# Second block of layer 2: a step's seven products of w_ch1 in one go, then all 36 matmuls of w_ch2

## The chip, the core and the metric

The kernel runs on one core of a Trainium2 chip. The metric is the time of one execution in device microseconds (us). Engines are called PE (TensorE, the matrix engine; PEld its weight loads), DVE (VectorE), ACT (ScalarE), POOL (GpSimd) and SP (the queue that issues the DMAs).

## What is computed

A retention layer feeds a gated layer, whose result x feeds a plain one. The change lies in the last of the three:

```python
def _moe2_ref(x, g_ln, w_ch1, w_ch2):
    mu = np.mean(x, axis=-1, keepdims=True)
    var = np.mean((x - mu) ** 2, axis=-1, keepdims=True)
    xn = (x - mu) / np.sqrt(var + 1e-06) * g_ln
    ch = np.maximum(xn @ w_ch1, 0.0) @ w_ch2
    return (x + ch).astype(np.float32)
```

x is (4, 576, 512), w_ch1 is 512 by 2048 and w_ch2 is 2048 by 512, all in float32.

## The kernel before

The 2304 rows of x are worked off in NB = 3 blocks of TB = 6 row tiles (768 rows). A block has NQ = 8 steps; a step makes 256 of the 2048 hidden columns. Steps are counted through, s = 0 to 23: block 0 is steps 0 to 7, block 1 steps 8 to 15, block 2 steps 16 to 23.

Precision comes from splitting each float32 operand into a high and a low part of type fp32r; `mm3` (lines 135 to 137) multiplies them in three matmuls, high by high, high by low, low by high.

*The products of a step.* xn @ w_ch1 is formed by a scheme with seven products in place of eight (`HIDDEN`: the features' mixture, the accumulator, and whether the product is the first or last of it). One call of `product` is one of them: two times `mm3`, six matmuls of 384 columns. Between them DVE and ACT add and subtract what has come out, in the tiles `u` and `t`, and `relu` (line 1173) makes the four quarters of the hidden tile `h`: ACT writes the high part (line 1175), DVE the low part (line 1176). Quarter (i, hh) is number q = 2 i + hh. `hidden(s)` issues the seven products in four parts, (0, 5), (1, 2), (3, 4) and (6,), and yields behind each.

*The projection.* `project(s, q)` multiplies quarter q by w_ch2: three row tiles times `mm3`, nine matmuls of 512 columns, called a portion here, 36 in four portions for a step. They add into six PSUM banks that hold the block's output rows for its eight steps. Of the eight banks two are left for products; `bank()` takes the one that has been free longest. At the block's last step DVE adds the residual row (loaded by `load_rest`) and SP stores the row.

*The order.* The main loop runs over s and, within it, over q = 0 to 3. In each turn stand: a part of step s's products, then one portion of the step before (so steps 1 to 16 hold 36 matmuls of w_ch2 in four portions), then the loading, splitting (`split_w2`, `split_w1`), saving (`save_w2`, `save_w1`) and fetching (`fetch_w1`) of weights, then `ahead`, the work on the next block: loading rows, normalising them (`norm`), loading them turned (`load_features`), scaling them (`scale_features`, ACT line 1015), and, in its turns 24 to 31, the differences (`mix_features`, POOL line 1029) and splits (`split_features`, ACT line 1036 and POOL line 1037) that make the mixtures. A turn of `ahead` is called a tick; `ahead` has 32 in a block. From step 8 on `turning` also brings w_ch2 into the form that block 2 wants: POOL differences (line 961), ACT casts into staging tiles (line 964), POOL low parts (line 967), and SP saves them (line 970).

Block 2 (`hidden_kept`) keeps its hidden tiles and is not projected step by step. Each engine carries out its instructions in the order in which this code issues them; nothing reorders them.

Of the kernel before, what the change touches and what calls it, by code (L numbers as in the profile page):

```python
# [27 lines left out]
KE = E // 128  # L28
# [73 lines left out]
def kernel(  # L102
# [1070 lines left out]
    def relu(s, i, v):  # L1173
        t = h_t[s, i] = h_at[i][s % len(h_at[i])]
        act.activation(out=t[:, 0], in_=v, func=ACTF.Relu)  # L1175
        dve.scalar_tensor_tensor(  # L1176
            out=t[:, 1], in0=v, scalar=0.0, in1=f(t[:, 0]), op0=ALU.max, op1=ALU.subtract
        )

    def hidden(s):  # L1180
# [5 lines left out]
        for part in ((0, 5), (1, 2), (3, 4), (6,)) if s else ((5, 0, 2, 4), (1,), (3,), (6,)):  # L1186
            for w in part:
# [7 lines left out]
                elif w in (0, 5):  # L1195
                    dve.tensor_tensor(out=u, in0=v, in1=u, op=ALU.add)
                elif w == 2 or w == 4:
                    dve.tensor_tensor(out=t, in0=v, in1=u if w == 2 else t, op=ALU.add)
                    if w == 4:
                        relu(s, 3, t)  # L1200
                else:
                    if w != 1:
                        y = u if w == 6 else v
                        dve.tensor_tensor(out=y, in0=v, in1=u, op=ALU.add)  # L1204
                        v = y
                    relu(s, {1: 0, 3: 2, 6: 1}[w], v)
                if last:
                    free(bk[a])
            yield

    def hidden_kept(s):
# [46 lines left out]

    def project(s, q):

        blk, p = divmod(s, NQ)
        i, h = divmod(q, 2)
        t = h_t.pop((s, q))
        if p == 0 and q == 0:
            o_t[blk] = [bank() for j in range(TB)]
        first, last = p == 0 and i == 0, p == NQ - 1 and i == 1
        w = w2_at[i]
        for j in reversed(range(TB // 2)):
            c = slice(j * 128, (j + 1) * 128)
            ps = o_t[blk][h * TB // 2 + j]  # L1270
            mm3(ps, t[:, 0, c], t[:, 1, c], w[:, 0], w[:, 1], first, last)
            if last:
                n = blk * TB + h * TB // 2 + j

                o = row_tile()
                dve.tensor_tensor(
                    out=turned_row(o), in0=ps.rearrange("p (f k c) -> p f k c", k=KE, c=32),
                    in1=o_s.pop(n).rearrange("p (f k c) -> p f k c", k=KE, c=32), op=ALU.add,
                )
                free(ps)  # L1280
                store_row(n, o)

# [111 lines left out]
    def ahead(blk, q):  # L1394
# [3 lines left out]
        n = (blk + 1) * TB  # L1398
        if q == 1 and blk:
            for j in reversed(range(TB // 2, TB)):  # L1400
                load_rest((blk - 1) * TB + j)
        if blk + 1 < NB:
# [21 lines left out]
            if q >= 24 and q != 28:  # L1424
                if q > 24:
                    next(feat[0], None)
                next(feat[1])
        if q == 4 * NQ - 1:
            for j in reversed(range(TB // 2)) if blk + 1 < NB else range(TB):
                load_rest(blk * TB + j)  # L1430
            if blk + 1 == NB:
                o_s[None] = row_tile()

# [29 lines left out]
    for s in range(NB * NQ):  # L1463
        if s == NK:
            keep()
        steps = hidden(s) if s < NK else hidden_kept(s)
        for q in range(4):
            next(steps)
            if 0 < s <= NK:
                project(s - 1, q)  # L1470
            if s >= NQ:
                next(turns, None)

            if q == 0 and s > 1:
                split_w2(2 * s - 1)
            if q == 1 and s > 1:
                load_w2(2 * s + 1)
                save_w2(2 * s - 1)
            if q == 2 and s:
                split_w2(2 * s)  # L1480
            if q == 3 and s:
                load_w2(2 * s + 2)
                save_w2(2 * s)
            if s and q == 2:
# [24 lines left out]
            else:  # L1509
                fetch_w1(s + 2, q - 1)  # L1510
    for _ in multiply_kept(NB - 1):
        pass
# [60 lines left out]
```

## Time and profile before

| | |
|---|---|
| median of 3 runs | 657.69 us (656.92 to 658.03) |
| the profiled execution | 658.18 us, its span 656.2 us |
| PE busy | 646.8 us, 99% of the span |
| DVE, ACT, POOL busy | 455.0, 316.0, 321.6 us |
| block 0 of layer 2 in the span | about 282 to 399 us, its last portions of w_ch2 in step 8 |
| block 1 | about 399 to 525 us, its last 36 matmuls of w_ch2 in step 16, to 541 us |

The span is cut into stretches for reading. A matmul's printed length reaches from its start to its modelled end and overlaps the next one, so the distance from start to start is what it costs. "Idle before" names what an engine waited for before an instruction. A DMA's time is from its issue on SP to its landing.

### The profile page before, as it was taken

To read this page: it belongs to the slowest core of one execution; us is meant where nothing else is said; L and a number is where in the kernel's file an instruction comes from. 1 tells how busy PE (TensorE), PEld (TensorE's weight loads), DVE (VectorE), ACT (ScalarE), POOL (GpSimd) and SP (SyncE) were. 2 spreads that over 40 slices of the span, in tenths; PEclk is the share of its full clock that TensorE was granted. 3 is DMA by queue.
4 is the path that set the end of the run, shared out by engine and by line. 5 is a ranking of instruction groups with operands and counts; after the bars stand their busy time and mean duration, and the time that the engine had idled before them with its cause. 6 is when DMAs were issued, how large, how long until landed. Compare 5 with 4: busy or idle time off the path is not lost.

```text
span 656.2 us, 12551 instructions
## 1 busy us (share of the span) xinstructions
PE 646.8 (99%) x4422; PEld 591.2 (90%) x4422; DVE 455.0 (69%) x906; ACT 316.0 (48%) x656; POOL 321.6 (49%) x315
## 2 busy tenths in 40 slices
PE   8998999999999999999999999999999999999997
PEld 5998899899889889899888999888988899999996
DVE  4698779789989885868888533555533345458894
ACT  4556795365286466434453533233535313335443
POOL 2467868225326528945655793265559743310000
PEclk9999999999999999999999999999999999999999
DMA  8999447777797695489896867799999699999634
GB/s 306 383 368 371 166 111 213 252 238 233 259 298 232 189 242 145 151 312 384 319 309 238 274 205 261 247 366 387 347 332 360 216 295 350 371 379 405 243 129 161
DMA packets 99264, 181.22 MB, mean 276 GB/s; under 512 B 9857, under 2 KB 46849, under 8 KB 97410
## 3 DMA queue, kind: packets, MB, share of 16 engines
q1 hardware_dynamic: 99202, 180.42, 81.5%
q8 instruction: 35, 0.57, 0.3%
q14 instruction: 27, 0.22, 0.1%
HBM read 122.97 MB, written 56.62 MB: 274 GB/s over the span
## 4 chain that ended last, share of the span: by engine, by line
PE 71%; DVE 3%; ACT 3%; DMA 1%; issue 1%; POOL 1%; SPq 0%; POOLq 0%; ACTq 0%; DVEq 0%
PE b L137 20%; PE b L136 20%; PE b L135 20%; PE b L864 4%; PE b L1341 3%; PE b L1342 2%; DVE c L163 1%; DMA raw<-in_w_ch_dram 1%; ACT t L695 1%; PE b L798 1%; POOL vnl L721 1%; PE b L797 0%; ACT t L692 0%; ACT raw L160 0%; DVE bs L669 0%
## 5 line engine op out<-in xcount | busy, mean ns | idle before, releaser
L137 PE MATMUL b<-fe,w 128*128 128x384 f32 x336 | 113.1, 337 | 0.0
L135 PE MATMUL b<-fe,w 128*128 128x384 f32 x336 | 112.9, 336 | 0.0
L136 PE MATMUL b<-fe,w 128*128 128x384 f32 x336 | 112.7, 335 | 0.0
L137 PE MATMUL b<-w,h 128*128 128x512 f32 (+1 forms) x270 | 98.1, 363 | 0.0
L136 PE MATMUL b<-w,h 128*128 128x512 f32 (+1 forms) x270 | 98.0, 363 | 0.0
L135 PE MATMUL b<-w,h 128*128 128x512 f32 (+1 forms) x270 | 96.8, 358 | 0.0
L945 POOL TENSOR_TENSOR w<-raw_w,w 128x512 fp32r<-128x512 f32 x30 | 39.6, 1320 | 59.0 <-ACT w L944 53.3
L135 PEld LDWEIGHTS b<-fe,w 128*128 128x128 f32 x336 | 63.1, 188 | 3.0
L136 PEld LDWEIGHTS b<-fe,w 128*128 128x128 f32 x336 | 63.1, 188 | 2.8
L137 PEld LDWEIGHTS b<-fe,w 128*128 128x128 f32 x336 | 63.0, 188 | 0.0
L137 PEld LDWEIGHTS b<-w,h 128*128 128x128 f32 x270 | 51.0, 189 | 7.6
L160 ACT ACTIVATE raw<-raw 128x512 f32<-128x512 f32 x44 | 29.9, 679 | 56.2 <-DVE b L158 49.3
L136 PEld LDWEIGHTS b<-w,h 128*128 128x128 f32 x270 | 50.9, 189 | 6.3 <-POOL w L945 0.2
L135 PEld LDWEIGHTS b<-w,h 128*128 128x128 f32 x270 | 51.0, 189 | 6.0 <-issue 0.2
L1175 ACT ACTIVATE h<-b 128x384 fp32r<-128x384 f32 x32 | 15.7, 492 | 83.8 <-DVE b L1204 54.1
L665 POOL TENSOR_TENSOR st<-st,par 128x1 f32<-128x1 f32 x36 | 22.1, 617 | 52.7 <-DVE st L664 52.2
L1176 DVE SCALAR_TENSOR_TENSOR h<-b,h 128x384 fp32r<-128x384 f32 x32 | 17.8, 556 | 30.9 <-ACT h L1175 30.9
L137 PE MATMUL b<-w_sg,vnl 128*128 128x288 f32 x128 | 37.8, 295 | 0.2 <-POOL vnl L721 0.2
L135 PE MATMUL b<-w_sg,vnh 128*128 128x288 f32 x128 | 37.8, 295 | 0.0
L137 PE MATMUL b<-xt_hi,w_in 128*128 128x288 f32 x128 | 37.7, 295 | 0.0
L136 PE MATMUL b<-w_sg,vnh 128*128 128x288 f32 x128 | 37.7, 295 | 0.0
L136 PE MATMUL b<-xt_lo,w_in 128*128 128x288 f32 x128 | 37.7, 294 | 0.0
(199 smaller groups left out, 1700.8 us busy)
## 6 DMA issues: line engine op xcount, KB each, us to landing
w<-ws_dram SPq DMA_DIRECT2D x96, 256.0 KB, 4.8
raw<-in_w_ch_dram SPq DMA_DIRECT2D x32, 512.0 KB, 5.0
ws_dram<-w SPq DMA_DIRECT2D x16, 896.0 KB, 7.4
w<-wb_dram SPq DMA_DIRECT2D x14, 1024.0 KB, 5.6
qv<-in_attn_dram SPq DMA_DIRECT2D x15, 576.0 KB, 6.8
w_dram<-c SPq DMA_DIRECT2D x32, 256.0 KB, 3.1
wb_dram<-fe SPq DMA_DIRECT2D x32, 256.0 KB, 5.1
kk<-in_attn_dram SPq DMA_DIRECT2D x15, 544.0 KB, 7.7
```

The source lines that it names most:

```text
L135: pe.matmul(ps, lh, rh, start=first, stop=False, skip_group_check=True)
L136: pe.matmul(ps, lh, rl, start=False, stop=False, skip_group_check=True)
L137: pe.matmul(ps, ll, rh, start=False, stop=last, skip_group_check=True)
L160: act.activation(out=f(w1), in_=f(w1), func=ACTF.Square)
L163: dve.scalar_tensor_tensor(out=f(c), in0=f(w1), scalar=F64_LEAST ** 2, in1=f(r), op0=ALU.is_ge, op1=ALU.mult)
L665: pool.tensor_tensor(out=st[:, 4:5], in0=st[:, 3:4], in1=col(par, O_MH), op=ALU.pow)
L864: pe.matmul(ps, g, wo[k][:, w], start=done[0] == 1, stop=done[0] == 3 * KE, skip_group_check=True)
L945: pool.tensor_tensor(out=t[:, 1], in0=raw, in1=f(t[:, 0]), op=ALU.subtract)
L1175: act.activation(out=t[:, 0], in_=v, func=ACTF.Relu)
L1176: dve.scalar_tensor_tensor(out=t[:, 1], in0=v, scalar=0.0, in1=f(t[:, 0]), op0=ALU.max, op1=ALU.subtract)
L1341: pe.matmul(ps, e[:, 0, x], t, start=begin, stop=False, skip_group_check=True)
L1342: pe.matmul(ps[:, 0:256], e[:, 1, x], t[:, 0:256], start=False, stop=end, skip_group_check=True)
```

## The change

In block 1 a step's seven products are issued in one go (`hidden_once`, in the order w = 0, 5, 1, 2, 4, 3, 6), and all 36 matmuls of w_ch2 of the same step behind them, quarters 3, 2, 0, 1. Within a quarter the nine matmuls run over the three row tiles for each of the three high and low pairs, where `mm3` did the three pairs for each row tile; the block's last step keeps `mm3`. The low part of `h` becomes a function of its own (`relu_low`), so that it may come later; for quarter 0 DVE first copies the product to a new tile `z`, and the bank is given back. The products of step 7 are projected behind step 7's last turn, so that step 8 starts with nothing left over, and step 16 has nothing to project. w_ch2's two splits of a step stand behind its second product and in the third turn, its loads and one of its saves behind the second product. The residual rows are loaded in ticks 28 and 29 (before: three in tick 31 and three in tick 1 of the next block). The work of the four turns, `ahead` included, is issued behind the portions as before, but a turn holds no products any more.

The number of matmuls and of DMAs is the same; DVE has eight copies more.

```diff
     def relu(s, i, v):
         t = h_t[s, i] = h_at[i][s % len(h_at[i])]
         act.activation(out=t[:, 0], in_=v, func=ACTF.Relu)
+
+    def relu_low(s, i, v):
+        t = h_t[s, i]
         dve.scalar_tensor_tensor(
             out=t[:, 1], in0=v, scalar=0.0, in1=f(t[:, 0]), op0=ALU.max, op1=ALU.subtract
         )
...
+    def hidden_once(s):
+        u = t2.tile([128, TH], F32, tag="u", name="u")
+        t = t2.tile([128, TH], F32, tag="v", bufs=1, name="t")
+        z = t2.tile([128, TH], F32, tag="z", bufs=1, name="z")
+        bk = {}
+        for w in (0, 5, 1, 2, 4, 3, 6):
+            x, a, first, last = HIDDEN[w]
+            if first:
+                bk[a] = bank()
+            product(s, bk[a], w, x, first, last)
+            v = bk[a][:, 0:TH]
+            if w == 0:
+                act.copy(u, v)
+            elif w == 1:
+                relu(s, 0, v)
+                dve.tensor_copy(out=z, in_=v)
+            elif w == 2 or w == 4:
+                dve.tensor_tensor(out=t, in0=v, in1=u if w == 2 else t, op=ALU.add)
+                if w == 4:
+                    relu(s, 3, t)
+            elif w == 3:
+                dve.tensor_tensor(out=v, in0=v, in1=u, op=ALU.add)
+                relu(s, 2, v)
+                relu_low(s, 3, t)
+            else:
+                dve.tensor_tensor(out=u, in0=v, in1=u, op=ALU.add)
+                if w == 6:
+                    relu(s, 1, u)
+            if last and w != 3:
+                free(bk[a])
+            if w == 5:
+                yield
+        relu_low(s, 2, bk[2][:, 0:TH])
+        free(bk[2])
+        relu_low(s, 0, z)
+        relu_low(s, 1, u)
+        yield
...
-    def project(s, q):
+    def project(s, q, begin=0):
...
-        first, last = p == 0 and i == 0, p == NQ - 1 and i == 1
+        first, last = p == 0 and i == begin, p == NQ - 1 and i != begin
         w = w2_at[i]
-        for j in reversed(range(TB // 2)):
+        js = list(reversed(range(TB // 2)))
+        for x, y in ((0, 0), (0, 1), (1, 0)) if begin and not last else ():
+            for j in js:
+                pe.matmul(
+                    o_t[blk][h * TB // 2 + j], t[:, x, j * 128:(j + 1) * 128], w[:, y], start=first and x == y,
+                    stop=False, skip_group_check=True,
+                )
+        for j in () if begin and not last else js:
...
-        if q == 1 and blk:
-            for j in reversed(range(TB // 2, TB)):
-                load_rest((blk - 1) * TB + j)
+        if q in (28, 29) and blk + 1 < NB:
+            for j in reversed(range(TB // 2)):
+                load_rest(blk * TB + (q - 28) * TB // 2 + j)
...
-        steps = hidden(s) if s < NK else hidden_kept(s)
+        if s < NQ:
+            steps = hidden(s)
+        elif s < NK:
+            steps = hidden_once(s)
+            next(steps)
+            split_w2(2 * s)
+            if s == NQ:
+                split_w2(2 * s + 1)
+            load_w2(2 * s + 2)
+            load_w2(2 * s + 3)
+            if s > NQ:
+                save_w2(2 * s + 1)
+            next(steps)
+        else:
+            steps = hidden_kept(s)
         for q in range(4):
-            next(steps)
-            if 0 < s <= NK:
+            if NQ <= s < NK:
+                project(s, (3, 2, 0, 1)[q], 1)
+            else:
+                next(steps)
+            if 0 < s < NQ:
                 project(s - 1, q)
             if s >= NQ:
                 next(turns, None)
 
-            if q == 0 and s > 1:
-                split_w2(2 * s - 1)
...
+            if s < NQ:
+                if q == 0 and s > 1:
+                    split_w2(2 * s - 1)
...
+            else:
+                if q == 1:
+                    save_w2(2 * s)
+                    if s == NQ:
+                        save_w2(2 * s + 1)
+                if q == 2:
+                    split_w2(2 * s + 3)
...
+        if s == NQ - 1:
+            split_w2(2 * s + 1)
+            load_w2(2 * s + 3)
+            for q in range(4):
+                project(s, q)
```

How the order moves, at three places. First PE, at the end of step 8 of block 1 before (b are PSUM banks, fe the features, w_3466 and w_3467 the high and low part of w_ch1, w_3373 the tile of w_ch2): the last three matmuls of a portion and the first three of the next product.

```order
L135 MATMUL b_76<-w_3373,h 128x512
L136 MATMUL b_76<-w_3373,h 128x512
L137 MATMUL b_76<-w_3373,h 128x512
L135 MATMUL b_78<-fe,w_3466 128x384 [waits DMAHW0_49]
L136 MATMUL b_78<-fe,w_3466 128x384
L137 MATMUL b_78<-fe,w_3467 128x384 [waits DMAHW1_49]
```

Now, at the end of the products of the first such step: the last three matmuls of the seventh product and the first nine of the 36.

```order
L135 MATMUL b_81<-fe,w_3371 128x384
L136 MATMUL b_81<-fe,w_3371 128x384
L137 MATMUL b_81<-fe,w_3372 128x384
L1316 MATMUL b_77<-w_3373,h 128x512 [waits Activation_49]
L1316 MATMUL b_78<-w_3373,h 128x512
L1316 MATMUL b_80<-w_3373,h 128x512
L1316 MATMUL b_77<-w_3373,h 128x512 [waits Pool_49]
L1316 MATMUL b_78<-w_3373,h 128x512
L1316 MATMUL b_80<-w_3373,h 128x512
L1316 MATMUL b_77<-w_3373,h 128x512 [waits DVE_49]
L1316 MATMUL b_78<-w_3373,h 128x512
L1316 MATMUL b_80<-w_3373,h 128x512
```

Behind a product stood nine matmuls of w_ch2 four times a step; now 36 stand together once.

Second DVE, in a step of block 1 before: from the sum for w = 5 to the sum for w = 6.

```order
L1196 TENSOR_TENSOR u<-b_78,u 128x384 [waits PE_49,Activation_49]
L1176 SCALAR_TENSOR_TENSOR h<-b_77,h 128x384 [waits Activation_49]
L1198 TENSOR_TENSOR t<-b_78,u 128x384 [waits DVE_49,PE_49]
L1204 TENSOR_TENSOR b_78<-b_78,u 128x384 [waits PE_49]
L1176 SCALAR_TENSOR_TENSOR h<-b_78,h 128x384 [waits Activation_49]
L1198 TENSOR_TENSOR t<-b_77,t 128x384 [waits DVE_49,PE_49]
L1176 SCALAR_TENSOR_TENSOR h<-t,h 128x384 [waits Activation_49]
```

The same piece now, to the end of the step's products.

```order
L1243 TENSOR_TENSOR u<-b_79,u 128x384 [waits PE_49,Activation_49]
L1233 COPY z<-b_81 128x384 [waits Activation_49]
L1235 TENSOR_TENSOR t<-b_79,u 128x384 [waits DVE_49,PE_49]
L1235 TENSOR_TENSOR t<-b_81,t 128x384 [waits DVE_49,PE_49]
L1239 TENSOR_TENSOR b_79<-b_79,u 128x384 [waits PE_49]
L1179 SCALAR_TENSOR_TENSOR h<-t,h 128x384 [waits Activation_49]
L1243 TENSOR_TENSOR u<-b_81,u 128x384 [waits DVE_49,PE_49]
L1179 SCALAR_TENSOR_TENSOR h<-b_79,h 128x384 [waits Activation_49]
L1179 SCALAR_TENSOR_TENSOR h<-z,h 128x384
L1179 SCALAR_TENSOR_TENSOR h<-u,h 128x384 [waits Activation_49]
```

The copy to z (L1233) is new, waits for ACT and reads b_81, the bank that w = 1 left and that w = 4 takes two products later (the row with t<-b_81,t); the low parts (L1179) stand later.

Third ACT, before, in the ticks 24 to 27 of block 1: the casts of the mixtures (L1036) up to the copy to u that begins step 15 (L1194).

```order
L1036 CAST fe<-x 128x768
L1175 ACTIVATE h<-b_79 128x384 [waits PE_49,Activation_49]
L1036 CAST fe<-mix 128x768 [waits Pool_49]
L1175 ACTIVATE h<-b_78 128x384 [waits DVE_49]
L1175 ACTIVATE h<-t 128x384 [waits DVE_49]
L944 CAST w_3373<-raw_w_5411 128x512 [waits DMAHW2_49,DMAHW3_49,PE_49,Activation_49]
L1036 CAST fe<-mix 128x768 [waits Pool_49]
L1175 ACTIVATE h<-u 128x384 [waits DVE_49,Activation_49]
L1036 CAST fe<-mix 128x768 [waits Pool_49]
L1194 COPY u<-b_78 128x384 [waits PE_49]
```

The same ticks now, from the last ReLU of step 14 to the first of step 15 (L1230 is the copy to u).

```order
L1175 ACTIVATE h<-u 128x384 [waits DVE_49,Activation_49]
L1036 CAST fe<-x 128x768
L1036 CAST fe<-mix 128x768 [waits Pool_49]
L944 CAST w_3373<-raw_w_5497 128x512 [waits DMAHW3_49,DMAHW2_49,DMAHW4_49,PE_49,Activation_49]
L1036 CAST fe<-mix 128x768 [waits Pool_49] x2
L1230 COPY u<-b_81 128x384 [waits PE_49]
L944 CAST w_3373<-raw_w_5495 128x512 [waits DMAHW3_49,DMAHW1_49,Activation_49]
L1175 ACTIVATE h<-b_81 128x384 [waits DVE_49,PE_49,Activation_49]
```

The four casts stood between the step's own ReLUs; now all four stand in a row in front of the next step's copy to u. On POOL the instructions behind the first of them are:

```order
L1037 TENSOR_TENSOR fe<-x,fe 128x768 [waits Activation_49]
L1029 TENSOR_TENSOR mix<-x,mix 128x768 [waits Pool_49]
L1037 TENSOR_TENSOR fe<-mix,fe 128x768 [waits Activation_49]
L945 TENSOR_TENSOR w_3373<-raw_w_5497,w_3373 128x512 [waits DMAHW3_49,DMAHW4_49,DMAHW2_49,Activation_49]
L1029 TENSOR_TENSOR mix<-x,mix 128x768 [waits Pool_49]
L1037 TENSOR_TENSOR fe<-mix,fe 128x768 [waits Activation_49]
```

The second difference (the lower L1029) is what the last of the four casts waits for.

## Rows read from the trace of the kernel before

**Rows 1.** The page, busy time of each engine

```profile
PE 646.8 (99%) x4422; PEld 591.2 (90%) x4422; DVE 455.0 (69%) x906; ACT 316.0 (48%) x656; POOL 321.6 (49%) x315
```

**Rows 2.** Timeline of PE, a step of block 1: start us, length us, instruction

```profile
407.64 0.33 PE L135 MATMUL b<-fe,w 128*128 128x384 f32 x1
...
408.70 0.33 PE L135 MATMUL b<-fe,w 128*128 128x384 f32 x1
...
409.74 0.39 PE L135 MATMUL b<-w,h 128*128 128x512 f32 x1
...
411.82 0.33 PE L135 MATMUL b<-fe,w 128*128 128x384 f32 x1
```

**Rows 3.** Timeline of PE, end of the layer before

```profile
279.31 2.88 PE L864 MATMUL b<-w_out,grem 128*128 128x512 f32 x12
282.03 0.33 PE L135 MATMUL b<-fe,w 128*128 128x384 f32 x1
```

**Rows 4.** Timeline of PE, at its one gap in the stretch

```profile
425.69 0.50 PE L136 MATMUL b<-w,h 128*128 128x512 f32 x1
426.03 0.40 PE L137 MATMUL b<-w,h 128*128 128x512 f32 x1
```

**Rows 5.** Timelines of PE and ACT in block 2, a product and its ReLU

```profile
550.98 0.33 PE L137 MATMUL b<-fe,w 128*128 128x384 f32 x1
551.35 0.49 ACT L1229 ACTIVATE kept<-b 128x384 f32<-128x384 f32 x1 [1.48 <-PE b L137]
```

**Rows 6.** Groups by line, 405 to 530 us: instruction, count, busy us, mean ns, idle before

```profile
L1175 ACT ACTIVATE h<-b 128x384 fp32r<-128x384 f32 x16 | 7.9, 492 | 51.1 <-DVE b L1204 30.4 <-PE b L137 20.7
L1175 ACT ACTIVATE h<-u 128x384 fp32r<-128x384 f32 x8 | 4.2, 526 | 7.6 <-DVE u L1204 7.6
L1204 DVE TENSOR_TENSOR u<-b,u 128x384 f32<-128x384 f32 x8 | 4.4, 550 | 2.9 <-PE b L137 2.9
L1037 POOL TENSOR_TENSOR fe<-mix,fe 128x768 fp32r<-128x768 f32 x4 | 7.7, 1923 | 0.0
L1037 POOL TENSOR_TENSOR fe<-x,fe 128x768 fp32r<-128x768 f32 x3 | 5.8, 1957 | 0.0
L1029 POOL TENSOR_TENSOR mix<-x,mix 128x768 f32<-128x768 f32 x2 | 3.7, 1840 | 0.0
L945 POOL TENSOR_TENSOR w<-raw_w,w 128x512 fp32r<-128x512 f32 x16 | 20.7, 1297 | 34.7 <-ACT w L944 28.9 <-DMA z_dram<-row 5.2 <-DMA w<-ws_dram 0.5
```

**Rows 7.** Timeline of ACT, 487 to 530 us

```profile
490.15 1.32 ACT L964 CAST fe<-raw_turn 128x256 fp32r<-128x256 f32 x4
491.38 0.62 ACT L944 CAST w<-raw_w 128x512 fp32r<-128x512 f32 x1
...
493.71 2.14 ACT L1015 ACTIVATE x<-x,par 128x384 f32<-128x384 f32 x4 [0.81 <-DMA x<-z_dram]
...
506.37 0.83 ACT L1036 CAST fe<-mix 128x768 fp32r<-128x768 f32 x1
...
509.68 0.84 ACT L1036 CAST fe<-mix 128x768 fp32r<-128x768 f32 x1 [1.06 <-POOL mix L1029]
510.58 0.48 ACT L1194 COPY u<-b 128x384 f32<-128x384 f32 x1
```

**Rows 8.** Timeline of POOL, 424 to 515 us

```profile
424.35 1.29 POOL L945 TENSOR_TENSOR w<-raw_w,w 128x512 fp32r<-128x512 f32 x1
...
511.85 1.84 POOL L1029 TENSOR_TENSOR mix<-x 128x768 f32<-128x768 f32 x1
513.65 1.84 POOL L1037 TENSOR_TENSOR fe<-mix,fe 128x768 fp32r<-128x768 f32 x1
```

**Rows 9.** Busy us in a stretch: PE, PEld, DVE, ACT, POOL, PEclk, DMA share, GB/s

```profile
437.00:501.00 64.00, 64.00 (x319) 57.55 (x318) 30.32 (x71) 28.21 (x59) 38.85 (x45) 1.00 1.06 361
```

**Rows 10.** Lines 970 (saves, 405 to 530 us) and 1007 (loads, 440 to 530 us)

```profile
DMA to landing us min/median/max: 5.1/5.2/6.3
...
DMA to landing us min/median/max: 4.3/5.4/6.6
```

More of the change, by code (lines that the diff above doesn't have):

```diff
@@ L1206, in hidden @@
                     relu(s, {1: 0, 3: 2, 6: 1}[w], v)
+                    relu_low(s, {1: 0, 3: 2, 6: 1}[w], v)
                 if last:
@@ L1209, in hidden @@
             yield
+    def hidden_once(s):
[21 more added lines that the diff above has]
+                relu(s, 2, v)
+                relu_low(s, 3, t)
+            else:
[11 more added lines that the diff above has]
+        yield
     def hidden_kept(s):
@@ L1263, in project @@
         t = h_t.pop((s, q))
-        if p == 0 and q == 0:
+        if blk not in o_t:
             o_t[blk] = [bank() for j in range(TB)]
-        first, last = p == 0 and i == 0, p == NQ - 1 and i == 1
+        first, last = p == 0 and i == begin, p == NQ - 1 and i != begin
         w = w2_at[i]
-        for j in reversed(range(TB // 2)):
+        js = list(reversed(range(TB // 2)))
[6 more added lines that the diff above has]
+        for j in () if begin and not last else js:
             c = slice(j * 128, (j + 1) * 128)
@@ L1271, in project @@
             mm3(ps, t[:, 0, c], t[:, 1, c], w[:, 0], w[:, 1], first, last)
[L1272 to L1281, printed above, removed]
+            if not last:
+                continue
+            n = blk * TB + h * TB // 2 + j
+            o = row_tile()
+            dve.tensor_tensor(
+                out=turned_row(o), in0=ps.rearrange("p (f k c) -> p f k c", k=KE, c=32),
+                in1=o_s.pop(n).rearrange("p (f k c) -> p f k c", k=KE, c=32), op=ALU.add,
+            )
+            free(ps)
+            store_row(n, o)
     def load_rest(n):
@@ L1427, in ahead @@
                 next(feat[1])
-        if q == 4 * NQ - 1:
-            for j in reversed(range(TB // 2)) if blk + 1 < NB else range(TB):
+        if q == 4 * NQ - 1 and blk + 1 == NB:
+            for j in range(TB):
                 load_rest(blk * TB + j)
-            if blk + 1 == NB:
-                o_s[None] = row_tile()
+            o_s[None] = row_tile()
     def keep():
@@ L1472 @@
                 next(turns, None)
-            if q == 0 and s > 1:
-                split_w2(2 * s - 1)
[L1476 to L1483, printed above, removed]
+            if s < NQ:
+                if q == 0 and s > 1:
+                    split_w2(2 * s - 1)
+                if q == 1 and s > 1:
+                    load_w2(2 * s + 1)
+                if q == 2 and s:
+                    split_w2(2 * s)
+                if q == 3 and s:
+                    load_w2(2 * s + 2)
+            else:
[5 more added lines that the diff above has]
+                    split_w2(2 * s + 3)
             if s and q == 2:
```

## The prediction

> **What bounds the kernel now.** The page comes first [rows 1]: the matrix engine (PE) is busy for 646.8 us, 99% of the span; its granted clock in the stretch of the change is 1.00, the 2.4 GHz level [rows 9]. Little can be won by waiting less. What is left is PE's pace, so the second view is PE's timeline, where the start of one matmul to the start of the next is the real price (the printed length overlaps the next one).
>
> A step of block 1 before the change is four parts of products (12, 12, 12 and 6 matmuls of 384 columns), each followed by a portion of nine matmuls of 512 columns. Twelve 512-column matmuls in undisturbed row take 282.03 - 279.31 = 2.72 us [rows 3], 0.227 each, so nine should take 2.04 us. The portion that starts at 409.74 ends at 411.82: 2.08 us [rows 2]. Six 384-column matmuls take 1.04 us in undisturbed row (408.70 to 409.74), but the six that follow a portion take 1.06 to 1.07 (407.64 to 408.70) [rows 2]. So one pair of shape switches costs 0.04 + 0.027 = 0.067 us, in a stage in which PE waits for nothing. The only gap that I found in the stretch is at 425.69: the next start comes 0.34 us later instead of 0.23 [rows 4], 0.11 lost.
>
> **The change part by part.**
>
> *1. Fewer switches.* Before, steps 8 to 16 hold 9 x 4 = 36 portions with a switch on either side. Afterwards steps 8 to 15 hold one group of 36 matmuls each, and the products of step 7 are projected right behind step 6's last portion, without a switch: 8 pairs. 28 x 0.067 = **1.9 us saved**. That 36 matmuls in a row pay the 0.04 once is taken from rows 2 and 3. The number of matmuls is the same; the other order inside a group (three banks in turn) is taken as free. The gap of 0.11 goes too, since that split of w_ch2 now stands a product earlier than its use: **0.1 saved**.
>
> The Trainium skill, "TensorE: Matmul & The Clock Gate", section "Back-to-back issue gap", gives N / 2.4 + 2.5 ns from the columns N alone, whatever stands in front; by it a switch is free and this term is nil. Rows 2 disagree with that here, and the rows decide.
>
> *2. A new wait inside the products.* Two PSUM banks are free for products while six hold the output rows. In the new order (w = 0, 5, 1, 2, 4, 3, 6) the fifth product, w = 4, takes the bank of the third, w = 1, one product after it was finished. Before it may start, ScalarE must do its ReLU out of that bank and then VectorE the new copy to z, one behind the other (the order shows the copy waiting for ScalarE). If S is the start of w = 2: w = 1 lands at S - 0.17 + 0.33 = S + 0.16; ScalarE starts 0.04 later (550.98 + 0.33 against 551.35) [rows 5] and takes 0.49 [rows 6]; VectorE starts after the same 0.04; the copy takes C; PE starts 0.05 after its releaser (424.35 + 1.29 against 425.69) [rows 4, 8]. That is S + 0.78 + C, where PE wants S + 1.04. No row shows this copy. VectorE's pass over 384 columns of PSUM takes 0.55 [rows 6], and ScalarE's copy of the same data 0.48 [rows 7]; I take 0.55, the engine's own: 0.29 late. Step 8 has more free banks, so it happens in 7 steps: 7 x 0.29 = **2.0 us lost** (1.5 with 0.48; nothing from a C of 0.26 down, less than half of any row).
>
> A rule of the Trainium skill, "PSUM — Partial Sum Buffer", section "PSUM bank collisions raise a hardware error", says that no two engines may read one bank at a time, so the copy could not run beside the ReLU; no run here shows that.
>
> *3. ScalarE's queue in front of the next step.* Everything that `ahead` spreads over the four ticks of a step now stands in one batch behind the step's products, and in front of the next step's copy to u, without which PE cannot put w = 1 onto w = 0. The worst batch is step 14's (ticks 24 to 27): four casts of features (L1036), three of them waiting for GpSimd's differences. Before, three matmul portions lay between these casts, and the copy followed the last one at no cost [rows 7]. Now, with Z the start of the projection: the last product lands at Z + 0.16, VectorE adds 0.55, ScalarE's ReLU 0.53, with two hand-overs Z + 1.3; the first cast 0.83 less 0.1 of overlap (490.15 + 1.32 against 491.38) [rows 7], Z + 2.0. Then GpSimd's queue as the order shows it: low part 1.96, difference 1.84, low part 1.92, w_ch2 split 1.30, difference 1.84 [rows 6], less four overlaps of 0.04 (511.85 + 1.84 against 513.65) [rows 8] and with one hand-over: Z + 10.8. Cast 0.83 and the copy 0.48 less 0.1: Z + 12.0, PE 0.05 later. PE is there at Z + 36 x 0.227 + 0.04 + 1.07 + 1.04 = Z + 10.3. **1.75 us lost**, 1.4 to 2.5 with the spread of GpSimd's rows. Step 15's batch has only one cast that waits for GpSimd, so it hides.
>
> *4. The same queue and the transfers.* In steps 11 to 13 the batch holds, before the copy to u, casts into staging tiles whose last save must have landed (L964 after `wb_dram<-fe`) and the scaling of features loaded in the same batch (L1015 after `x<-z_dram`). Before, the load and its use lay three ticks, some 12 us, apart; still ScalarE once waited 0.81 [rows 7]. From 437 to 501 us the DMA engines are full (share 1.06) [rows 9], and a save takes 5.1 to 6.3 us and these loads 4.3 to 6.6 from issue to landing [rows 10]. From the ReLU's end to the moment the copy is due ScalarE has about 10.3 - 1.3 = 9 us, of which its own work takes 1.32 for four casts, 0.62 for w_ch2, 2.14 for four scalings and 0.48 [rows 7], 4.6. So 4.4 us of a landing are covered and up to 6.6 - 4.4 = 2.2 are not, in two steps (12 to 13, 13 to 14). Bounds: 0, if SP issues early enough, to 4.4. The engines are full in just this stretch, so I take the middle and a little more: **2.5 us lost**.
>
> *5. What I cost at nothing.* Eight VectorE copies and the late low halves: VectorE is at about half [rows 9], and each low half is due later than it is made: z's low half is made about 2 us after the products, and PE needs it some 5 us after. The split of w_ch2 behind step 7 (0.62 + 1.30) has the first 18 matmuls, 4.1 us, as cover. VectorE's six row additions for block 0 come in a lump, beside 8.2 us of matmuls. The residual rows are loaded two or three ticks earlier and all DMAs keep their number. If GpSimd is late with these splits, PE waits at once for the second group of a projection; I found no place where it is.
>
> **Sum.** -1.9 - 0.1 + 2.0 + 1.75 + 2.5 = +4.3 us. Against the profiled execution, 658.18 us (span 656.2 and 2.0 around it), that is 662.5. The median of the runs shown is 0.5 lower than this execution, so the forecast is **662.0 us**.
>
> **Rivals.**
> *A, the waits hide (faster).* PE keeps the 2.0 us of the switches, if the z copy takes under 0.26 us and GpSimd's chain in step 14 is 1.75 us shorter than worked out: 657.7 - 2.0 = 655.7. For it: PE waits for nothing now. Against: both chains are sums of rows, and the covers that they had, the portions, are what the change takes away. It decides where the chain of part 2 stays under 1.04 us. Chance 0.12.
> *B, they cancel.* Term 2 comes as said, terms 3 and 4 hide, because ScalarE's queue has more air than I think: -2.0 + 2.0, 657.7. Chance 0.15.
> *C, only what needs no transfer.* Terms 1 to 3 without 4: -2.0 + 3.75, 659.5. For it: the bound of 0 in part 4. Chance 0.2.
> *D, switches are free.* Grouping saves nothing and the waits come: 657.7 + 2.0 + 1.75 + 2.5 = 664. Chance 0.05. This is what the TensorE page's formula would give.
> *The forecast*, all four terms, 660.5 to 664.5 by the bounds of part 4: 0.48.
>
> **How the numbers follow.** About 0.2%, 1.3 us, is what a measurement can tell from no change. Faster is A, 0.12; the same is B, 0.15; slower are C, D and the forecast, 0.73. For 8 in 10 the range leaves out A and a part of B at the lower end, and the sum with part 4 at its upper bound stays in: 657.5 to 664.5.
>
> **What would show it.** Right: in steps 9 to 15 a gap of 0.2 to 0.3 us in front of the fifth product, with VectorE as releaser; a gap of about 1.8 us in front of the third product of step 15, with ScalarE as releaser and GpSimd's L1029 behind it; smaller ones of that kind one and two steps earlier, with transfers behind ScalarE; 36 projection matmuls in about 8.20 us. Wrong: step lengths of 15.5 us throughout block 1 (before, 15.7) mean A; no gaps and 15.7 mean D without its waits; large gaps at projection matmuls, released by GpSimd, would be a wait that I cost at nothing.

## The result and the profile after

The changed kernel takes 667.37 us (median of 6, 665.61 to 668.79), the kernel before 657.86 in the same series: a ratio of 1.0141, 95% interval 1.0117 to 1.0166. It is slower, by 9.5 us where 4.3 were forecast, and lies 2.9 us above the range. The profiled execution, from which all that follows is read, took 667.75 us with a span of 666.0, against 658.18 and 656.2 before.

The first lines of its page: busy time of each engine, and the granted clock of PE in 40 slices.

```profile
PE 649.5 (98%) x4422; PEld 592.5 (89%) x4422; DVE 455.6 (68%) x914; ACT 317.1 (48%) x656; POOL 320.1 (48%) x315
...
PEclk9999999999999999999999999999997999999999
```

Beside [rows 1] hardly a number has moved, and that is the first thing to learn here: nearly 10 us are lost and PE's share falls by one point. Only one slice, with its clock at 7 tenths, says where to look.

So the stretch is cut into steps, by the first product of each. From the start of layer 2 to the end of step 16's products it was 258.70 us before; now:

```profile
280.14:550.50 270.36, 262.04 (x1291) 235.12 (x1290) 148.11 (x294) 105.53 (x194) 148.72 (x133) 0.99 0.87 291
```

11.66 us more. The layers before happen to end 1.89 us earlier in this execution than in the one of [rows 3] (over the profiled executions of this study layer 2 begins between 280.0 and 283.0 us, with the same code in front of it), which is why the spans differ by 9.8 only. The steps 8 to 15, one per row (columns: stretch, its length, busy us of PE, PEld, DVE, ACT, POOL, PEclk, DMA share, GB/s):

```profile
405.52:421.02 15.50, 15.50 (x79) 14.06 (x78) 6.48 (x12) 4.18 (x8) 3.83 (x3) 1.00 0.85 269
421.02:436.99 15.97, 15.81 (x79) 14.04 (x78) 7.58 (x21) 4.87 (x11) 7.34 (x10) 1.00 0.86 274
...
468.93:484.91 15.98, 15.81 (x79) 14.04 (x78) 9.38 (x26) 5.77 (x11) 8.27 (x12) 1.00 1.08 326
484.91:503.64 18.73, 16.11 (x80) 14.03 (x78) 6.25 (x11) 7.92 (x17) 9.93 (x12) 1.00 1.00 335
503.64:525.44 21.80, 18.43 (x79) 16.68 (x78) 5.21 (x10) 7.96 (x14) 11.62 (x10) 0.84 0.92 293
525.44:543.20 17.76, 16.09 (x80) 14.00 (x78) 7.97 (x15) 5.96 (x10) 14.62 (x9) 1.00 0.61 192
```

Step 8 is what the change was to be everywhere: 15.50 us for the 15.705 of before (125.64 for eight steps). Steps 9 to 12 take 0.47 more than that, steps 13, 14 and 15 take 3.2, 6.3 and 2.3 more. Together 13.7 us; less the 2.0 that the switches and the one gap give back, 11.7.

What PE waited for, from 405 to 545 us (total us, times, longest):

```profile
PE b L135 <- ACT u L1230: 7.3, 3, 3.4
PE b L135 <- DVE z L1233: 1.0, 6, 0.2
```

There are just two kinds of wait, and both were named in the prediction. Their places in PE's timeline: the 36 matmuls of step 8, the wait for z in step 9, those for u in steps 14 and 15.

```profile
412.82 8.36 PE L1316 MATMUL b<-w,h 128*128 128x512 f32 x36
421.02 0.33 PE L135 MATMUL b<-fe,w 128*128 128x384 f32 x1
...
425.06 0.34 PE L137 MATMUL b<-fe,w 128*128 128x384 f32 x1
425.56 0.45 PE L135 MATMUL b<-fe,w 128*128 128x384 f32 x1 [0.15 <-DVE z L1233]
425.84 0.34 PE L136 MATMUL b<-fe,w 128*128 128x384 f32 x1
...
505.57 0.34 PE L137 MATMUL b<-fe,w 128*128 128x384 f32 x1
509.27 0.69 PE L135 MATMUL b<-fe,w 128*128 128x384 f32 x1 [3.37 <-ACT u L1230]
...
527.38 0.34 PE L137 MATMUL b<-fe,w 128*128 128x384 f32 x1
529.20 0.45 PE L135 MATMUL b<-fe,w 128*128 128x384 f32 x1 [1.49 <-ACT u L1230]
```

Read starts, not lengths. The 36 matmuls take 421.02 - 412.82 = 8.20 us, as forecast. The wait for z shows as 0.15, but from start to start it costs 425.56 - 425.06 = 0.50 where 0.17 is usual, and the matmul behind it comes 0.28 later where 0.17 is usual: 0.33 of waiting and 0.11 of starting again. In step 14 the start comes 3.70 later, 3.53 too late, and then the matmuls themselves are slower:

```profile
509.27:514.88 5.61, 5.61 (x17) 5.61 (x18) 1.66 (x3) 0.96 (x2) 3.05 (x2) 0.50 0.91 310
```

For 5.61 us behind the gap the granted clock is 0.50, the 1.2 GHz level; a matmul of 384 columns then takes 0.32 us for 0.17, which costs 2.8 us with the restart. The Trainium skill, "TensorE: Matmul & The Clock Gate", section "Part 1: The HAM clock gate (the "warmup" mystery)", says that the clock is halved when the engine has lately been idle; this row agrees.

### The profile page after: what moved, and what is told of

It reads as the page before. It is cut to its first block, busy times and chain, and to the rows that moved or that the text cites. A ratio compares the mean times of both kernels' runs of the same rounds, so it can differ in the third digit from the quotient of the medians.

```text
span 666.0 us, 12551 instructions
## 1 busy us (share of the span) xinstructions
PE 649.5 (98%) x4422; PEld 592.5 (89%) x4422; DVE 455.6 (68%) x914; ACT 317.1 (48%) x656; POOL 320.1 (48%) x315
## 5 line engine op out<-in xcount | busy, mean ns | idle before, releaser
L135 PE MATMUL b<-fe,w 128*128 128x384 f32 x336 | 114.9, 342 | 8.3 <-ACT u L1230 7.3
L137 PE MATMUL b<-fe,w 128*128 128x384 f32 x336 | 113.9, 339 | 0.0
L136 PE MATMUL b<-fe,w 128*128 128x384 f32 x336 | 113.7, 338 | 0.0
L135 PEld LDWEIGHTS b<-fe,w 128*128 128x128 f32 x336 | 64.0, 190 | 12.9 <-ACT u L1230 8.3
L945 POOL TENSOR_TENSOR w<-raw_w,w 128x512 fp32r<-128x512 f32 x30 | 39.4, 1315 | 70.0 <-ACT w L944 42.6
L136 PEld LDWEIGHTS b<-fe,w 128*128 128x128 f32 x336 | 63.9, 190 | 1.5
L137 PEld LDWEIGHTS b<-fe,w 128*128 128x128 f32 x336 | 63.9, 190 | 0.0
L1316 PE MATMUL b<-w,h 128*128 128x512 f32 x270 | 62.8, 390 | 0.0
L137 PE MATMUL b<-w,h 128*128 128x512 f32 (+1 forms) x180 | 62.3, 346 | 0.0
L136 PE MATMUL b<-w,h 128*128 128x512 f32 (+1 forms) x180 | 62.2, 346 | 0.0
L135 PE MATMUL b<-w,h 128*128 128x512 f32 (+1 forms) x180 | 61.8, 343 | 0.0
L1316 PEld LDWEIGHTS b<-w,h 128*128 128x128 f32 x270 | 50.6, 188 | 10.2
L137 PE MATMUL b<-xt_hi,w_in 128*128 128x288 f32 x128 | 37.7, 295 | 0.0
L137 PEld LDWEIGHTS b<-w,h 128*128 128x128 f32 x180 | 34.1, 189 | 4.1
L135 PE MATMUL b<-xt_hi,w_in 128*128 128x288 f32 x128 | 37.7, 294 | 0.0
L135 PEld LDWEIGHTS b<-w,h 128*128 128x128 f32 x180 | 34.1, 189 | 3.5 <-issue 0.2
```

Of the source, the lines that this page charges most:

```text
L135: pe.matmul(ps, lh, rh, start=first, stop=False, skip_group_check=True)
L136: pe.matmul(ps, lh, rl, start=False, stop=False, skip_group_check=True)
L137: pe.matmul(ps, ll, rh, start=False, stop=last, skip_group_check=True)
L945: pool.tensor_tensor(out=t[:, 1], in0=raw, in1=f(t[:, 0]), op=ALU.subtract)
L1316: pe.matmul(o_t[blk][h * TB // 2 + j], t[:, x, j * 128:(j + 1) * 128], w[:, y], start=first and x == y, stop=False, skip_group_check=True,)
```

## Behind the long gaps

ScalarE's timeline in front of the copy to u (L1230) of steps 13, 14 and 15:

```profile
480.02 0.81 ACT L692 ACTIVATE row<-row,st 128x512 f32<-128x512 f32 x1
485.65 0.41 ACT L964 CAST fe<-raw_turn 128x256 fp32r<-128x256 f32 x1 [4.83 <-DMA wb_dram<-fe]
...
488.39 0.81 ACT L692 ACTIVATE row<-row,st 128x512 f32<-128x512 f32 x1
489.11 0.46 ACT L1230 COPY u<-b 128x384 f32<-128x384 f32 x1
...
506.73 2.13 ACT L1015 ACTIVATE x<-x,par 128x384 f32<-128x384 f32 x4 [4.68 <-DMA x<-z_dram]
508.77 0.46 ACT L1230 COPY u<-b 128x384 f32<-128x384 f32 x1
...
523.10 0.84 ACT L1036 CAST fe<-mix 128x768 fp32r<-128x768 f32 x1 [0.87 <-POOL mix L1029]
527.94 0.83 ACT L1036 CAST fe<-mix 128x768 fp32r<-128x768 f32 x1 [4.01 <-POOL mix L1029]
528.68 0.47 ACT L1230 COPY u<-b 128x384 f32<-128x384 f32 x1
```

In step 13 it sat 4.83 us for saves out of the staging tiles, in step 14 4.68 us for loads of features, in step 15 4.01 us for GpSimd. The issues of those saves and loads on SP (start, time of issuing, count), and from issue to landing:

```profile
478.27 1.62 SPq L951 DMA_DIRECT2D wb_dram<-w  x2
480.31 2.32 SPq L970 DMA_DIRECT2D wb_dram<-fe  x4
...
495.25 2.70 SPq L970 DMA_DIRECT2D wb_dram<-fe  x4
498.00 2.81 SPq L1007 DMA_DIRECT2D x<-z_dram  x4
```

```profile
DMA to landing us min/median/max: 4.3/6.0/6.3
```

The last load is issued at 500.3 and lands at 506.6. The last ReLU of that step ended at 496.9, so SP was 3.4 us behind ScalarE when it issued, with the four saves in front; the prediction had counted landing from the ReLU's end. Not all of this is the issuing of transfers. SP's waits from 485 to 501 us have this row:

```profile
SPq L939 <- POOL w L945: 2.0, 1, 2.0
```

For 2.0 us SP stood in front of a load of w_ch2 (L939) until GpSimd's split (L945) was done, and everything behind it stood too. On GpSimd that split (from 492.58) stands behind the low parts (L967) of what step 13's late casts had written, so the lateness of step 13 pushed back the loads of step 14 too.

## The experiments

"Block 1" is the profiled length of steps 8 to 15, first product to first product: 125.64 us before, 137.68 after; eight steps like step 8 would be 124.06. Medians of a few executions scatter by 1 to 2 us here, so a mechanism is judged by this length and by PE's waits, the worth of a version by its ratio. e2 has the edits of e1 and e4 together. e7 to e12 build on e2: e7 has e6's edit beside it, e8 has e5's, and e10 also has e9's; the code below shows what each adds.

| run | median us | ratio (interval) | block 1 us |
|---|---|---|---|
| before | 657.8 | 1 | 125.64 |
| the change | 667.37 | 1.0141 (1.0117 to 1.0166) | 137.68 |
| e1_z_first | 666.26 | 1.0130 (1.0100 to 1.0159) | 134.44 |
| e2_z_first_u_on_dve | 661.60 | 1.0060 (1.0040 to 1.0080) | 127.72 |
| e3_scale_next_step | 668.07 | 1.0157 (1.0138 to 1.0175) | 136.87 |
| e4_u_on_dve | 664.85 | 1.0105 (1.0086 to 1.0123) | 132.16 |
| e5_early_save | 669.23 | 1.0182 (1.0151 to 1.0213) | 138.17 |
| e6_turn_later | 676.53 | 1.0288 (1.0253 to 1.0323) | 130.11 |
| e7_z_u_turn_later | 672.36 | 1.0232 (1.0199 to 1.0266) | 124.08 |
| e8_z_u_early_save | 661.83 | 1.0072 (1.0044 to 1.0100) | 129.98 |
| e9_norm_early | 662.16 | 1.0067 (1.0041 to 1.0093) | 129.91 |
| e10_norm_loads_early | 660.91 | 1.0053 (1.0033 to 1.0072) | 129.28 |
| e11_tick_behind_third_product | 661.11 | 1.0073 (1.0046 to 1.0101) | 129.44 |
| e12_turn_spread | 660.78 | 1.0043 (1.0028 to 1.0058) | 124.06 |

**e1_z_first**: is it the chain ReLU, copy that holds the bank?

```diff
-                relu(s, 0, v)
                 dve.tensor_copy(out=z, in_=v)
+                relu(s, 0, z)
```

> VectorE copies the product to z first and ScalarE's ReLU reads z, so the bank comes free after one pass instead of two. Theory (the chain ReLU, then copy, then bank sets the wait in front of w = 4; a restart of PE costs some 0.14 us on top): the copy ends 0.8 us behind the start of w = 2, before PE wants the bank at 1.04, so all seven waits of 0.46 us go, 3.2 us in all, 667.4 to 664.2. Rival (VectorE's queue or another reader holds the bank): less than 1 us gained. The long gaps of steps 13 to 15 stay in both.

PE's waits, 405 to 545 us:

```profile
PE b L135 <- ACT u L1230: 8.0, 3, 3.6
```

The wait for z is gone in all six steps, and steps 9 to 12 now take 15.51 to 15.54 us. The chain is the cause. Block 1 is 3.24 us shorter, as expected to the tenth, but that is luck: steps 9 to 12 and 15 give 2.2, step 13 gives nothing (18.77 us for 18.73), because its wait for u grows by 0.55, and 1.05 comes from step 14, where there was no wait for z and the low clock now ends sooner. The median shows 1.1 of the 3.24.

**e4_u_on_dve** and **e2_z_first_u_on_dve**: are the long gaps ScalarE's queue?

```diff
             if w == 0:
-                act.copy(u, v)
+                dve.tensor_copy(out=u, in_=v)
```

> Only the copy to u goes to VectorE; z is still copied behind ScalarE's ReLU. Theory: w = 1 starts on time, but the ReLU of w = 1 still stands behind ScalarE's batch, so the lateness comes back in front of w = 4, smaller by the two products between (2.1 us) and larger by ReLU and copy (1.2) and the split of w_ch2 (0.6): some 1.9, 2.7 and 0.8 us in steps 13, 14, 15 for 2.9, 3.7 and 2.2 now, and less of the low clock: 667.4 to some 664 to 665 without the clock's share, 662 with it. Rival (the long gaps came from the place of the copy alone): three gaps gone, 657.

> As e1_z_first, and VectorE instead of ScalarE makes the copy to u, so nothing that PE waits for inside the products stands behind ScalarE's batch. Theory (the three long gaps are ScalarE's queue alone): 3.2 us and the three gaps of steps 13, 14, 15 with the lowered clock behind the second (2.8 + 5.8 + 1.8 us) go: 667.4 - 13.6 + 2 for what is late next, 654 to 656. Rival (ScalarE's lateness only moves: its ReLUs come late to the 36 matmuls of the same step): gaps of 1 to 3 us at the first matmuls of w_ch2 in steps 13 to 15, 658 to 662.

e4: 5.5 us less in block 1 (2.5 in the median), near the 5.4 that the theory gave with the clock's share, but not in its places, so the match is luck. The gaps of steps 14 and 15 go nearly whole (0.34 and 0.70 us are left, at w = 4, where 2.7 and 0.8 were said); step 13's stays at 3.2, where 1.9 was said. e2: 10.0 us less; that one gap is left, beside 0.4 us at the projection of step 14, and its releaser is VectorE:

```profile
PE b L135 <- DVE u L1230: 3.0, 1, 3.0
```

VectorE's timeline of e2 at that place:

```profile
488.54 0.71 DVE L994 STREAM_TRANSPOSE row<-row 128x512 f32<-128x512 f32 x1 [4.44 <-ACT row L692]
489.17 0.52 DVE L1230 COPY u<-b 128x384 f32<-128x384 f32 x1
```

The copy now stands behind the transpose of a row, that waits for ScalarE's L692, and L692 for the same casts L964 behind the same saves. So ScalarE's queue is the cause in all three steps, but in step 13 VectorE hangs on it too. The sum said 654 to 656, with 2 us for what is late next; steps 13 and 14 lose 3.7. Much of the rest lies outside block 1, which here begins 1.4 us later than in the changed kernel's execution. The profiled execution of e2 took 659.54, the median 661.60; what the other executions lost beyond it was not seen in a trace.

**e3_scale_next_step**: is step 14 the scaling behind its loads?

```diff
-            if q in (15 + blk, 22 + blk):
+            if q in (15 + blk, 22 + 2 * blk):
```

> The second half of the features is scaled one tick later (24 for 23), which is the next step's batch, so that its loads have a whole step to land; all else as in the changed kernel. Theory: the 3.5 us gap of step 14 goes, and with it the 18 products at the lower clock (2.65 us); step 15's gap of 1.65 us grows by up to the 2.1 us of the scaling, which now stands in front of the differences: 667.4 - 6.2 + 2.1 = 663.3. Rival 1 (the clock falls there for another reason than the gap): 667.4 - 3.5 + 2.1 = 666. Rival 2 (the copy to u waits for something else): no change.

Step 14's wait for u goes, 0.56 us in front of w = 4 is left, and its low clock goes too. In step 15 the gap grows by 2.06, as the 2.1 of the scaling said, to 3.7, and now the low clock follows there (at 528.61):

```profile
528.61 0.69 PE L135 MATMUL b<-fe,w 128*128 128x384 f32 x1 [3.54 <-ACT u L1230]
```

So the clock is the gap's doing. The time was 4.8 us above the one expected, since the clock's price moved along, and step 13 lost 0.7 us more: its gap was 0.3 shorter, but here the clock fell behind it (0.74 granted from 491.5 to 498 us).

**e5_early_save** and **e8_z_u_early_save**: does the order on SP decide?

```diff
-            for o in (0, 1, 1, 2, 2, 3, 4, 5):
+            for o in (0, 1, 1, 2, 2, 3, 4, 4 + p // 5):
```

> The changed kernel, the four saves of a turned tile of w_ch2 issued in the tick of its low parts, one tick earlier and so ahead of some nine other DMAs on SP's queue; nothing else. Theory (step 13's gap is ScalarE's casts L964 waiting for the saves out of the same staging tiles, step 14's is the scaling L1015 waiting for loads that SP issues behind the next four saves): the casts no longer wait; step 13 keeps what is late next, the normalising L692 behind GpSimd's L961 and L665, some 1.3 of 2.8 us; step 14's loads go out 2.5 us earlier, its gap falls from 3.5 to about 1 us and the clock stays up (2.65 us): 667.4 - 1.5 - 5.1 = 660.8. Rival (the DMA engines are full there, so whichever goes first the other lands late): under 2 us in all, 665.5 or more.

> e2_z_first_u_on_dve with the saves as in e5_early_save. Theory: step 13's gap falls from 3.3 to 1 to 2 us, the chain GpSimd L961, L665, ScalarE L692, VectorE L994 in front of the copy to u being next: 661.6 - 1.3 to 2.3 = 659 to 660.5. Rival (the saves are not what holds ScalarE): 661.6 unchanged.

No: block 1 is 0.5 us longer in e5, 2.3 in e8 (beside e2). The saves go out earlier (475.40 for 480.31) and the casts no longer wait for them. They wait for GpSimd's differences, and those for the load that now stands behind the saves, as ScalarE's and GpSimd's timelines of e5 show:

```profile
488.38 0.71 ACT L964 CAST fe<-raw_turn 128x256 fp32r<-128x256 f32 x2 [1.22 <-POOL raw_turn L961]
```

```profile
485.15 3.19 POOL L961 TENSOR_TENSOR raw_turn<-raw_turn 128x256 f32<-128x256 f32 x4 [9.00 <-DMA raw_turn<-w_dram]
```

The load is issued at 478.33, where it was 474.04. The rival of e5 was right: the DMA engines have no air there (share 1.00 to 1.08), and what one transfer gains another loses. The theory saw the next wait, behind GpSimd's L961, but not that the load behind the saves makes it as long as the one that goes.

**e6_turn_later** and **e7_z_u_turn_later**: is it the turning of w_ch2?

```diff
-            start, pace = (3 + 4 * p, 1) if p < 5 else (8 * p - 8, 2)
+            start, pace = (3 + 4 * p, 1) if p < 3 else (6 * p + 14, 1)
```

> The changed kernel, the turning of w_ch2 for its pieces 3 to 7 put into block 2 (32 ticks, one every six), so that ScalarE, GpSimd, SP and the DMA engines carry none of it in steps 12 to 15. Theory: step 13's gap goes whole (2.8 us); step 14's loads are issued 2.5 us earlier and have fuller DMA engines to themselves: gap under 1 us, no lower clock (5 us); step 15's gap, GpSimd's own chain, stays at 1.65: 667.4 - 7.8 = 659.6. Rival (lateness comes from the normalising chain and the loads alone): 3 us or less, 664.5; block 2 may lose up to 1 us to the turning in either case.

> e2_z_first_u_on_dve with the turning as in e6_turn_later. Theory: what was left in e2 (3.3 us in step 13, 0.4 at the projection of step 14) goes too, and only the grouping's gain of 1.9 us is left: 656 to 657, at or below the kernel before. Rival (block 2 pays for the turning, or step 13's normalising chain stays): 658 to 660.

In block 1, yes. In e6 step 13 has no wait for u any more, step 14's is 0.9 us with no low clock, step 15's the same 1.65. The features' loads of step 14 in e6 (the span of their issues, then from issue to landing):

```profile
L1007 SPq DMA_DIRECT2D x<-z_dram x4: 303/396/523, 495.8 to 497.8; - x4
...
DMA to landing us min/median/max: 5.9/7.0/7.2
```

The last is issued as the ReLU ends (497.8), 3.4 us sooner against it than in the changed kernel, and although it takes 7.2 us to land instead of 6.3, the gap falls from 3.5 to 0.9: what made it long was the late issue, not the landing. In e7 block 1 has no gap at all, 124.08 us, 1.56 less than before:

```profile
406.92:531.00 124.08, 124.08 (x625) 112.49 (x624) 64.44 (x143) 43.27 (x80) 59.47 (x56) 1.00 0.89 286
531.00:605.99 74.99, 63.37 (x338) 62.41 (x337) 31.56 (x57) 23.26 (x54) 29.10 (x41) 0.93 1.00 352
```

But the second row, the products of block 2, is 16.7 us longer than the 58.27 of the changed kernel (13.9 in e6): the casts L964 now stand in front of block 2's copies to u (L1270), and the clock falls there too. That price was set at 1 us or less and not worked out.

**e9_norm_early**, **e10_norm_loads_early**, **e11_tick_behind_third_product**: can step 13 be freed with the turning where it is?

```diff
-                at = 3 + 5 * j // 2
+                at = 3 + 5 * j // 2 - 2 * blk
```

> e2_z_first_u_on_dve with the rows of block 2 loaded and normalised two ticks earlier in block 1, so that in step 12 both normalisings L692 stand ahead of the casts L964 on ScalarE, and VectorE's transposes L994 behind them no longer wait for the saves. Theory (in e2 the copy to u on VectorE stood behind L994, that behind L692, that behind L964, that behind the saves of the staging tiles): the 3.3 us gap of step 13 goes, 661.6 - 3.3 = 658.3; step 11 may get a small one, since one L692 now stands behind its L964. Rival (the copy to u on VectorE is late for VectorE's or the matrix engine's own reasons): 661 or more.

In e9 step 13 is free of gaps, but step 11, where one L692 now stands behind its casts, has one of 2.3 us instead of a small one, and loses 4.0 with the low clock behind it; one of ScalarE's ReLUs comes 1.6 us late to step 14's projection. The mechanism holds, the place moves.

```diff
-            if q in (13, 20):
-                load_features(blk + 1, q // 20)
+            if q in (13 - blk, 20 - blk):
+                load_features(blk + 1, q // (20 - blk))
```

> As e9_norm_early, and the loads of the turned features one tick earlier, 12 and 19 for 13 and 20, which is a whole batch earlier for the second half. Theory (what was left in step 14 is the scaling L1015 waiting for loads that SP issues late in the same batch): the 0.4 us at the projection of step 14 goes too, and no gap above 0.3 us is left in block 1: 656 to 658. Rival (the earlier loads push the saves on SP's queue back and L964 is later still): a gap in step 13 of 2 us or more, 660 to 662.

Neither reading: step 13 stays free, yet 1.9 us are lost in step 11, 0.6 in step 12, 1.8 at the projection of step 14 and 0.8 at that of step 15.

```diff
             next(steps)
+            if s > NQ:
+                ahead(1, 4 * (s - NQ) - 1)
+            next(steps)
...
-            ahead(*divmod(4 * s + q, 4 * NQ))
+            if q < 3 or not NQ <= s < NK - 1:
+                ahead(*divmod(4 * s + q, 4 * NQ))
```

(with a second `yield` in `hidden_once` behind w = 1)

> e2_z_first_u_on_dve with the `ahead` work of a step's fourth turn issued behind the third product (w = 1) of the next step of block 1, so that in step 13 the transpose L994 no longer stands in front of VectorE's copies to u and z. The scaling of tick 23 and the cast of tick 27 move in the same way on ScalarE. Theory (step 13's gap in e2 is VectorE's queue: L994 behind L692 behind L964 behind the saves): L964, L692 and L994 are as late as before, 489.2, but what stands behind them is only VectorE's sum for w = 2, due at about 489.7: gap of 0.3 us or less instead of 3.3, 661.6 - 3.1 = 658.5, and 658 without the 0.4 at step 14's projection. Rival (the matrix engine is held by the hidden quarters that ScalarE then makes late): gaps of 1 to 2 us at the projection of steps 13 or 14, 660 to 661.

PE's waits in e11:

```profile
PE b L135 <- DVE t L1235: 2.2, 2, 1.9
PE b L1316 <- ACT h L1175: 1.9, 1, 1.9
```

The copy to u is on time, but the transpose comes at 490.29, not 489.2, and holds the sum for w = 2; and in step 14 the rival's wait comes, the projection on ScalarE's ReLU. In e2 steps 13 and 14 lose 3.7 us together, in e11 4.3: the lateness is about the same, and the order only chooses who meets it.

**e12_turn_spread**: e2 with the turning spread over block 2.

```diff
-            start, pace = (3 + 4 * p, 1) if p < 5 else (8 * p - 8, 2)
-            for o in (0, 1, 1, 2, 2, 3, 4, 5):
-                at.setdefault(start + o * pace, []).append(p)
+            start = 3 + 4 * p if p < 3 else 6 * p + 10
+            for o in (0, 1, 1, 2, 2, 3, 4, 5) if p < 3 else (0, 2, 2, 4, 4, 6, 7, 8):
+                at.setdefault(start + o, []).append(p)
```

> e2_z_first_u_on_dve with the pieces 3 to 7 of the turning in block 2 as in e7_z_u_turn_later, but one every six ticks with longer ways inside a piece: differences two and four ticks behind the load, casts at six, saves at eight, so that four ticks (7.3 us) lie between a save and the next casts into the same tiles, as the kernel before has it for its last three pieces. Theory (e7 lost its 13 us in block 2 to casts L964 behind saves that had just been issued, in front of ScalarE's copies L1270): block 1 stays free of gaps at 15.51 us a step, block 2 loses under 1 us: 656 to 657.5, the grouping's gain of 1.9 us at last to be seen. Rival (five pieces are more than the DMA engines carry in block 2 beside its own loads, however they are spread): gaps of 2 us or more in front of products in block 2, 660 to 668.

```profile
407.71:531.77 124.06, 124.06 (x625) 112.49 (x624) 64.57 (x143) 43.27 (x80) 59.31 (x58) 1.00 0.90 292
531.77:595.59 63.82, 60.40 (x337) 57.86 (x336) 31.29 (x57) 23.25 (x54) 29.26 (x40) 1.00 1.03 361
```

Block 1 is exactly eight times step 8, and the grouping's gain is there in full. Block 2 loses 5.6 us for it, its DMA share at 1.03, so the theory's price of under 1 us was wrong and the rival right: the longest wait there, 2.4 us, is again a copy to u behind casts L964 behind saves. Of the 13 versions this comes nearest to the kernel before and still is slower, 1.0043 (1.0028 to 1.0058). None beats it.

## Why the prediction was wrong, point by point

*Fewer switches, -1.9 and -0.1: right in size.* 36 matmuls in 8.20 us, and 15.50 for 15.705 in every step without a wait (step 8, and all eight in e12). The order of the nine matmuls inside a group is free, as taken. In the last step the first 18 of the 36 have the new order and only the last 18 keep `mm3`: 535.00 to 539.12 and 539.12 to 543.20, 4.12 and 4.08 us, and the 0.04 is the one switch. By the formula of the Trainium skill, "TensorE: Matmul & The Clock Gate", section "Back-to-back issue gap", nothing would have been saved; these rows stand against it, as [rows 2] did.

That it is the change of shape that costs the 0.067 is not shown, only that the boundary between the two groups does. In block 2 of the kernel before, 512 and 256 columns alternate:

```profile
606.34 0.40 PE L1341 MATMUL b<-w,h 128*128 128x512 f32 x1
606.58 0.28 PE L1342 MATMUL b<-w,h 128*128 128x256 f32 x1
606.69 0.40 PE L1341 MATMUL b<-w,h 128*128 128x512 f32 x1
```

A pair takes 0.35 us there, 0.227 and the 0.12 that 256 columns take in undisturbed row (650.98 to 651.46 for four), so two changes of shape cost less than 0.01. What in the boundary costs it stays open.

*The wait for the bank of w = 1, +2.0: mechanism right, size off by 0.8.* The chain was worked out at S + 1.33 and came at S + 1.39 (w = 2 starts at 424.17, w = 4 at 425.56); the copy takes 0.56 where 0.55 was taken, and the ReLU starts 0.05 later than in the sum. What is mainly missing is the price of starting again, 0.11 for the second matmul and 0.03 for the next ones. It was in the rows: in [rows 4] the second start comes 0.34 behind the first instead of 0.23, and the prediction charged that to the gap there and to no other. 0.47 in six steps is 2.8; in step 14 the slowed PE came late enough not to wait.

*Step 15 behind GpSimd's chain, +1.75: right.* The start came 1.65 late, 1.79 with the restart, released by the copy behind the last cast L1036 behind L1029.

*ScalarE behind transfers, +2.5 with an upper bound of 4.4: this step failed.* It measured 2.8 in step 13 and 6.3 in step 14, 9.1 in all. Two things were left out. The bound took the loads as issued when ScalarE was ready for them; they were issued 3.4 us later, because SP's queue carries the whole batch in its order and stood 2.0 of the 3.4 for GpSimd. From the ReLU's end to the moment PE was ready (505.74) there were 8.8 us, less 2.6 for the scaling and the copy; 3.4 of issue and 6.3 of landing are 3.5 more than that. (The prediction took off 4.6 for ScalarE's work; 2.0 of it ran while the loads were under way, an error the other way.) Step 13 adds up in the same manner: the last save was issued at 482.3, 4.2 us behind the ReLU's end, landed in 5.2, and from there to the end of the copy ScalarE needed 2.0, its normalising L692 among it, which the prediction did not count; of these 11.4 us 8.9 were covered, and the 2.5 that are left are the 2.6 by which PE's start came late. And it took a gap to cost its length; behind this one PE ran 5.6 us at half its clock, 2.8 us more, a term that no bound held. Steps 13 and 14 are where the prediction looked for the term; its size is what failed. With the terms as measured, -2.0 + 2.8 + 1.8 + 9.1, the sum is 11.7, the stretch's 11.66.

*What was costed at nothing* did cost nothing: no wait for GpSimd at the projection, none for VectorE's lumps, none for the splits.

The rivals: A and B fell with the waits; C had everything but the term that turned out the largest; D's time of 664 was the nearest, for a wrong reason.

## What to carry to other kernels

Grouping work on the engine that bounds a kernel also takes apart the spacing of everything that is issued between the groups: four ticks that lay 4 us apart became one batch, so a load and its use in one batch have no distance at all. Before such a change, follow each in-order queue (here SP, then ScalarE) through one batch from the issue of a transfer to its user, and count from the time at which the queue reaches the issue. And price a gap on PE with its restart and, for gaps of a few us, with the clock behind it; in step 14 the gap was 3.5 of 6.3 us. A gain of 0.2 us a step is not worth a chain that is short by a few us.

## What the runs showed of the hardware beyond that

The restart of PE costs the same 0.11 us behind gaps of 0.3 to 3.2 us that left the clock up, 0.28 to the second start for 0.17 (0.34 for 0.23 at 512 columns). The clock's fall isn't settled by the gap's length alone. It stood at 1.2 GHz (0.50 granted) from the first matmul behind 3.5 us in step 14 and behind 3.7 in e3, and from about a microsecond later, for a part of the step, behind 2.3 us in e9 and 3.2 in e4 (0.70 and 0.68 granted over the 5 to 6 us behind the gap), but not at all behind 3.2 in e1 and e2 (1.00).
